# Window attention and expert layer on one core: head loads into spare weight memory, two weight pieces in flight, and a new order of small work

## The chip, the core and the metric

The kernel runs on one core of a Trainium2 chip. The metric is the device time in microseconds (us) of one execution. The core's engines work in parallel, each on its own queue in order: TensorE (PE, matmuls and transposes), VectorE (DVE), ScalarE (ACT), GpSimd (POOL), and SyncE (SP), which here only loads registers and issues DMAs. ACT and POOL issue DMAs too.

## The reference, cut to what matters

Attention over 8 sequences of 576 positions, 8 heads of 64, in which a position sees itself and the 63 before it; its result, 4608 rows of 512, goes through a layer of 8 experts, of which each row uses one.

```python
def _attn_ref(q, k, v):                      # (8, 8, 576, 64)
    scores = (1 / np.sqrt(D)) * q @ k^T
    mask = (rel >= 0) & (rel < 64)           # rel = query position - key position
    attn = softmax(np.where(mask, scores, -1e9))
    return attn @ v

def _moe_ref(x, modality_id, w_gate, modality_bias, w1, w2):   # x (4608, 512)
    logits = x @ w_gate + modality_bias[modality_id]
    e_idx = np.argmax(logits, axis=1)
    gate_w = softmax(logits)[np.arange(N), e_idx]
    for e in range(8):
        h = np.maximum(x[mask_e] @ w1[e], 0)                   # w1[e] (512, 1024)
        out[mask_e] = gate_w[mask_e, None] * (h @ w2[e])       # w2[e] (1024, 512)
```

## The kernel before

**Steps.** The attention is worked through in 36 steps s, each for one pair of 64-row blocks (128 rows); two pairs are a group G. The loop at L917 writes each step out by hand for five engines (`manual_schedule`): what stands first in the loop stands first on its engine's queue. In step s PE does the router's logits of pair s-3, values of s-2, scores of s, transposes of the exponentials of s-1, the transposes of x of s-2, and the transposes of heads of a later group (`heads_t`, group s//2+1: the k heads in an even step, the q heads in an odd one). DVE takes the scores' masked minima (`minima`, L562), copies half of v (`swap_v`, L492), forms the reciprocal of the sums (`sums`, L589 and L590), copies most heads out, adds the bias (L629) and multiplies the values by the reciprocal (`values_out`, L607). ACT takes the exponentials (`exps`, L574, eight a step), copies pT (L583) and xaT (L616) and the second half of the k heads (L524). POOL copies the other half of v (L493) and scatters the finished rows by expert into memory (L700, an indirect DMA).

**Heads.** q and k of a group (512 KB each) are loaded by SP (`load_qk`, L509) into two buffers `qk`; k of group G in step 2G-3, q in 2G-2, used from step 2G-2 on. SP issues in order, so a load that waits for its buffer holds up what stands behind it. v of pair p (256 KB, three buffers) is loaded in step p.

**Table work.** The routing of rows to experts makes short DVE instructions. They stand in two lists, `routing` (of the current group) and `queue` (of the plan of which rows make up a slot), and `tick(n)` issues the next n entries, `routing` first. The third entry of a group's route also issues a small exp on ACT (L647). Each step has four ticks of 4 (of 10 in step 10). `choose` (step 5) picks the two experts whose weights are kept, `plan` (after groups 2, 4, 5, 6, 8, 10, 13, 15) appends 11 or 12 entries that end in the row number of a slot.

**Weights.** Each of two experts X and Y has 32 KB per partition in `Whi` and again in `Wlo`: a weight is split into a rounded part and its rest, and each product is made of three matmuls. `weights(s)` splits the piece loaded last (ACT or POOL copies it into Whi, L108; POOL subtracts into Wlo, L109) and loads the next of 32 pieces of 256 KB into one of two buffers `raw`. It is called once a step before step 12, three times from there on.

**Slots.** From step 12 (`FIRST`) on, pieces of expert work are put between the attention pieces, four `gap`s a step. A slot is 256 rows of one expert, in 16 pieces: `fetch` gets the row number and loads the rows (L196, tile `xt`), `x_part` transposes and splits them (L245, L185, L186), `first` makes the hidden layer (L270, k from 0 to 3), `second` the output (L292), `finish` the scaling (L300) and the indirect store (L303). The next slot is fetched at k == 3 of the current one while attention runs, at k == 2 after it.

Before the loop stand the setup of constants, the first group's heads (`first_heads`, two pairs of blocks i), and `keep_warm`, a few matmuls on zeros.

Of the kernel before, what the change touches and what calls it, by code (L numbers as in the profile page):

```python
# [26 lines left out]
def tile_window_attn_moe(  # L27
# [56 lines left out]

    Whi = wpool.tile([P, 2, 2 * WC], F32R, name="Whi")
    Wlo = wpool.tile([P, 2, 2 * WC], F32R, name="Wlo")

# [17 lines left out]
    def split_piece(raw, buf, c, lo_engine, hi_copy=nc.scalar.copy):  # L105

        cols = slice(c * WCH, (c + 1) * WCH)
        hi_copy(out=Whi[:, buf, cols], in_=raw)  # L108
        lo_engine.tensor_tensor(  # L109
            out=Wlo[:, buf, cols], in0=raw, in1=Whi[:, buf, cols].bitcast(F32), op=ALU.subtract)  # L110

# [120 lines left out]
    def slot_pieces():  # L232
# [26 lines left out]
        def first(sl, k, i):  # L259

            buf = sl["buf"]
            if i == 0:
                sl["hb"] = bank(k % 2)
            hb = sl["hb"]
            hi, lo = sl["x"]
            mm = [(w, c, hi) for c in range(NC1) for w in (Whi, Wlo)] + [(Whi, c, lo) for c in range(NC1)]
            for n, (w, c, x) in enumerate(mm):
                c0 = c * F + (2 * k + i) * P
                ready(sl, c0)
                nc.tensor.matmul(  # L270
                    out=hb[:, i * TP:(i + 1) * TP], lhsT=w[:, buf, c0:c0 + P], rhs=x[:, c * TP:(c + 1) * TP],
                    start=(n == 0), stop=(n == len(mm) - 1))
            if i == 1:
                hh = epool.tile([P, 512], F32R, name="hh", bufs=2)
                hl = epool.tile([P, 512], F32R, name="hl", bufs=2)
                sl["h", k] = hh, hl
                later.append(lambda: (
                    nc.scalar.activation(out=hh, in_=hb, func=AF.Relu),  # L278
                    nc.vector.scalar_tensor_tensor(  # L279
                        out=hl, in0=hb, scalar=0.0, in1=hh.bitcast(F32), op0=ALU.max, op1=ALU.subtract)))  # L280

        def second(sl, k, t):

            buf = sl["buf"]
            if k == 0:
                sl["y", t] = ps_m.tile([P, DM], F32, name=f"y{t}")
            hi, lo = sl["h", k]
            mm = [(h, w, i) for i in range(2) for h, w in ((hi, Whi), (hi, Wlo), (lo, Whi))]
            for n, (h, w, i) in enumerate(mm):
                c0 = WC + (2 * k + i) * DM  # L290
                ready(sl, c0)
                nc.tensor.matmul(  # L292
                    out=sl["y", t], lhsT=h[:, i * TP + t * P:i * TP + (t + 1) * P], rhs=w[:, buf, c0:c0 + DM],
                    start=(k == 0 and n == 0), stop=(k == NK - 1 and n == len(mm) - 1))
            if k == NK - 1:
                later.append(lambda: finish(sl, t))

        def finish(sl, t):
            y = epool.tile([P, DM], F32, name="y", bufs=2)
            nc.vector.tensor_scalar(  # L300
                out=y, in0=sl["y", t], scalar1=sl["gate"][:, t:t + 1], scalar2=None, op0=ALU.mult)
            nc.gpsimd.memset(pause, 0.0)
            ins = nc.gpsimd.indirect_dma_start(  # L303
                out=out, out_offset=bass.IndirectOffsetOnAxis(ap=sl["id"][:, t:t + 1], axis=0),
                in_=y, in_offset=None, bounds_check=N - 1, oob_is_err=False)
            tc.declare_no_dep(ins.ins, group="outs", reason="rows are distinct")
            tc.add_to_no_dep_group("outs", ins.ins)

        def half_first(sl, n):
# [5 lines left out]
            for m, (x, w, c) in enumerate(mm):  # L315
                c0 = c * F + n * 512
                ready(sl, c0)
                nc.tensor.matmul(
                    out=hb, lhsT=x[:, c * P:(c + 1) * P], rhs=w[:, buf, c0:c0 + 512],
                    start=(m == 0), stop=(m == len(mm) - 1))  # L320
# [13 lines left out]
        def half_second(sl, a):  # L334
# [5 lines left out]
            for m, (w, n, c, lo) in enumerate(mm):  # L340
# [3 lines left out]
                    out=yp[:, cols], lhsT=sl["h", n][lo][:, c * P:(c + 1) * P],  # L344
                    rhs=w[:, buf, c0 + cols.start:c0 + cols.stop],
                    start=(m == 0), stop=(m == len(mm) - 1))
# [5 lines left out]
            def out_():  # L352
                y = epool.tile([P, DM], F32, name="y", bufs=2)
                nc.vector.tensor_scalar(
# [104 lines left out]

    PARTS = ((K0, K1), (Q0, Q1))  # L460
    WARM = 4, 3

# [32 lines left out]
    def new_qk(G, nm):  # L495
        qk[G, nm] = work.tile([P, 2, H, D], F32, name="qk", bufs=2)

# [88 lines left out]
    def sums(p):  # L586
        sm = st[p, "s"][2]
        rs = st[p, "rs"] = small.tile([P, H], F32, name="rs")
        nc.vector.tensor_scalar(out=rs, in0=sm, scalar1=1e-9, scalar2=None, op0=ALU.add)  # L589
        nc.vector.reciprocal(out=rs, in_=rs)  # L590

# [194 lines left out]

    spare = epool.tile([P, DM], F32, name="y", bufs=2)
    mod_i = spare[0:NPR, 0:2 * P].bitcast(I32)
# [20 lines left out]
    nc.gpsimd.memset(kT[:, :, RING - 1, :], 0.0)  # L809
    warm = const.tile([1, 1], F32, name="warm")  # L810
    nc.vector.memset(warm, 0.0)
    nc.scalar.activation(out=warm, in_=warm, func=AF.Exp)

# [61 lines left out]
    padrow = epool.tile([P, 2, ROW], F32, name="xt")  # L875
    spare2 = epool.tile([P, DM], F32, name="y", bufs=2)
    nc.gpsimd.memset(padrow, 0.0)
# [21 lines left out]

    for i in range(GB):  # L900
        for nm in "kq":
            first_heads(nm, i, turn_bank(0), nc.vector.tensor_copy if nm == "k" else nc.scalar.copy)
        if i == 0:
            keep_warm(WARM[1])
    by_bias = []

    def weights(s):

        if raws:
            raw, x, c = raws.pop(0)  # L910
            split_piece(raw, x, c, nc.gpsimd, nc.scalar.copy if s >= FIRST else nc.gpsimd.tensor_copy)
        if pieces:
            x, c = pieces.pop(0)
            raw = epool.tile([P, WCH], F32, name="raw", bufs=2)
            raws.append((load_piece(raw, evs[x], c), x, c))

    for s in range(NPR + 4):  # L917
# [30 lines left out]
        run_later()  # L948
        tick(n_tick)
        if s < NPR:  # L950
# [31 lines left out]
        run_later()  # L982
        tick(n_tick)
        if s == 0:
# [277 lines left out]
```

## Time and profile before

| | us |
|---|---|
| median of 3 runs | 665.7 (664.6 to 666.95) |
| the profiled execution | 664.81 |
| its span | 663.1 |
| PE busy | 627.0 |
| DVE, ACT, POOL busy | 361.9, 298.1, 166.5 |

The span goes from the first to the last instruction on the core. A busy engine is one with an instruction under way; matmuls overlap, so a share of 95% isn't 95% of what PE could do. The rows in the next sections come from the page, from groups of instructions by line ("busy, mean ns of one | idle before"), from tables of waits ("engine, line waited for: us in total, times, longest us"), from the timeline ("start, length, engine, line, operation", and in brackets the idle time of the engine just before), from the chain of work that ended last, and from busy time by stage.

### The profile page before, as it was taken

The numbers are of one execution on the slowest core, as the hardware profiler recorded it, in microseconds if no ns is written. First come the engines' busy times: TensorE is split into PE (matmuls) and PEld (weight loads), VectorE is DVE, ScalarE is ACT, GpSimd is POOL, SyncE is SP. The second block draws the span as 40 slices with busy tenths as digits, with TensorE's granted clock in tenths as the row PEclk, the third lists the DMA queues.
The fourth block names the chain that finished last, engine by engine and source line by source line (L and its number), as shares of the span: only waits on it lengthen the run. The fifth ranks groups of instructions, "written<-read, shape, count | busy, mean of one in ns | idle before, by whom it ended". The sixth has DMA issues, their size and how long they took to land.

```text
span 663.1 us, 17266 instructions
## 1 busy us (share of the span) xinstructions
PE 627.0 (95%) x6508; PEld 559.6 (84%) x6508; DVE 361.9 (55%) x1465; ACT 298.1 (45%) x928; POOL 166.5 (25%) x314
## 2 busy tenths in 40 slices
PE   6887688899999999999999999999999999999996
PEld 4776578688888998999898988999999899999986
DVE  2689974657766676655765563222222634566611
ACT  2687747557666655455555111111111523555511
POOL 4303623535555032122230410110011011011102
PEclk9999988899999999999999999999999999999999
DMA  7957974666687463646422216411050651677400
GB/s 121 201 112 164 223 173 115 174 160 178 175 214 170 100 160 86 140 112 146 112 85 64 97 49 208 160 63 49 17 191 24 177 183 46 216 247 228 137 1 35
DMA packets 138885, 88.07 MB, mean 133 GB/s; under 512 B 116746, under 2 KB 116784, under 8 KB 138672
## 3 DMA queue, kind: packets, MB, share of 16 engines
q1 hardware_dynamic: 130112, 67.44, 41.8%
q0 software_dynamic: 5856, 18.92, 7.9%
q10 hardware_dynamic: 2832, 0.59, 0.7%
q8 instruction: 52, 0.85, 0.6%
q14 instruction: 33, 0.27, 0.1%
HBM read 67.49 MB, written 23.91 MB: 138 GB/s over the span
## 4 chain that ended last, share of the span: by engine, by line
PE 83%; DVE 5%; ACT 4%; DMA 4%; issue 2%; POOL 1%; SPq 1%; POOLq 0%; ACTq 0%; DVEq 0%
PE y L292 30%; PE em L270 20%; PE sp L270 10%; PE tp L430 8%; PE sp L548 5%; PE av L600 4%; PE tp L624 3%; ACT ss L574 2%; DMA qk<-in_k_dram 2%; DVE ss L562 2%; PE y L343 1%; PE em L245 1%; PE tp L245 1%; DMA xt<-xs_scratch 1%; DMA qk<-in_q_dram 0%
## 5 line engine op out<-in xcount | busy, mean ns | idle before, releaser
L292 PE MATMUL y<-Whi,hh 128*128 128x512 f32 x288 | 119.5, 415 | 0.7 <-ACT Whi L108 0.7
L292 PE MATMUL y<-Wlo,hh 128*128 128x512 f32 x288 | 113.7, 395 | 2.5 <-POOL Wlo L109 2.5
L292 PE MATMUL y<-Whi,hl 128*128 128x512 f32 x288 | 113.3, 394 | 0.0
L574 ACT ACTIVATE ss<-ss,mn 128x128 f32<-128x128 f32 x288 | 112.4, 396 | 1.8 <-DVE mn L562 1.8
L270 PE MATMUL em<-xh,Whi 128*128 128x256 f32 x392 | 101.7, 293 | 2.5 <-ACT xh L185 1.9
L270 PE MATMUL em<-xh,Wlo 128*128 128x256 f32 x392 | 96.8, 280 | 0.0
L303 POOL DMA_INDIRECT out_dram<-y,id x36 | 37.2, 1032 | 204.7 <-DVE y L300 167.1
L279 DVE SCALAR_TENSOR_TENSOR hl<-em,hh 128x512 fp32r<-128x512 f32 x49 | 33.8, 690 | 91.4 <-ACT hh L278 88.8
L270 PEld LDWEIGHTS em<-xh,Whi 128*128 128x128 f32 x392 | 74.4, 190 | 3.9 <-ACT xh L185 2.1
L270 PEld LDWEIGHTS em<-xh,Wlo 128*128 128x128 f32 x392 | 74.4, 190 | 0.9
L562 DVE CUSTOM_DVE_ANT_0 ss<-sp,masks 128x128 f32<-128x128 f32 x288 | 63.6, 286 | 14.7 <-PE sp L548 14.3
L583 ACT COPY pT<-tp 128x512 f32<-128x512 f32 x58 | 31.5, 590 | 83.7 <-PE tp L430 83.7
L278 ACT ACTIVATE hh<-em 128x512 fp32r<-128x512 f32 x49 | 29.0, 593 | 87.3 <-PE em L270 87.3
L292 PEld LDWEIGHTS y<-Whi,hl 128*128 128x128 f32 x288 | 54.4, 189 | 12.4
L292 PEld LDWEIGHTS y<-Wlo,hh 128*128 128x128 f32 x288 | 54.6, 190 | 10.6 <-POOL Wlo L109 3.5
L270 PE MATMUL em<-xl,Whi 128*128 128x256 f32 x392 | 62.3, 281 | 0.0
L292 PEld LDWEIGHTS y<-Whi,hh 128*128 128x128 f32 x288 | 54.4, 189 | 8.9 <-ACT Whi L108 1.4
L700 POOL DMA_INDIRECT xs_scratch<-xa,idx x36 | 35.5, 986 | 96.2 <-DVE idx L712 26.3
L574 ACT ACTIVATION_READ_ACCUMULATOR ss<-ss,mn 128x1 f32 x288 | 55.6, 193 | 0.0
L109 POOL TENSOR_TENSOR Wlo<-raw,Whi 128x512 fp32r<-128x512 f32 x32 | 41.0, 1281 | 51.5 <-ACT Whi L108 47.7
L270 PEld LDWEIGHTS em<-xl,Whi 128*128 128x128 f32 x392 | 53.1, 190 | 0.0
L279 DVE SCALAR_TENSOR_TENSOR hl<-sp,hh 128x512 fp32r<-128x512 f32 x23 | 15.9, 692 | 66.2 <-ACT hh L278 66.2
(233 smaller groups left out, 1277.6 us busy)
## 6 DMA issues: line engine op xcount, KB each, us to landing
xt<-xs_scratch SPq DMA_DIRECT2D x18, 514.0 KB, 4.2
vo<-in_v_dram SPq DMA_DIRECT2D x32, 256.0 KB, 5.1
raw<-in_moe_w_dram SPq DMA_DIRECT2D x32, 256.0 KB, 4.0
vo<-in_moe_w_dram SPq DMA_DIRECT2D x24, 256.0 KB, 3.6
ss<-in_moe_w_dram SPq DMA_DIRECT2D x24, 256.0 KB, 3.6
qk<-in_k_dram SPq DMA_DIRECT2D x22, 256.0 KB, 4.8
qk<-in_q_dram SPq DMA_DIRECT2D x22, 256.0 KB, 4.1
xs_scratch<-xs_scratch SPq DMA_DIRECT2D x8, 514.0 KB, 6.2
```

The lines of the kernel that those rows point to most:

```text
L109: lo_engine.tensor_tensor(out=Wlo[:, buf, cols], in0=raw, in1=Whi[:, buf, cols].bitcast(F32), op=ALU.subtract)
L270: nc.tensor.matmul(out=hb[:, i * TP:(i + 1) * TP], lhsT=w[:, buf, c0:c0 + P], rhs=x[:, c * TP:(c + 1) * TP], start=(n == 0), stop=(n == le ...
L278: nc.scalar.activation(out=hh, in_=hb, func=AF.Relu),
L279: nc.vector.scalar_tensor_tensor(out=hl, in0=hb, scalar=0.0, in1=hh.bitcast(F32), op0=ALU.max, op1=ALU.subtract)))
L292: nc.tensor.matmul(out=sl["y", t], lhsT=h[:, i * TP + t * P:i * TP + (t + 1) * P], rhs=w[:, buf, c0:c0 + DM], start=(k == 0 and n == 0), s ...
L303: ins = nc.gpsimd.indirect_dma_start(out=out, out_offset=bass.IndirectOffsetOnAxis(ap=sl["id"][:, t:t + 1], axis=0), in_=y, in_offset=None ...
L430: nc.tensor.transpose(out=out_, in_=in_, identity=ident[p0:p0 + n, p0:p0 + n])
L548: nc.tensor.matmul(out=sp[a][c * W64:(c + 1) * W64, hp * P:(hp + 1) * P], lhsT=qT[rows, hp, g + c, :], rhs=kT[rows, hp, win[c], :], start= ...
L562: nc.vector.tensor_tensor_reduce(out=ss[a][:, hp, :], in0=sp[a][:, hp * P:(hp + 1) * P], in1=mask, scale=-1.0 / 8.0, scalar=3.0e38, op0=AL ...
L574: nc.scalar.activation(out=ss[a][:, hp, :], in_=ss[a][:, hp, :], func=AF.Exp, bias=mn[:, h:h + 1], scale=-1.0, accum_out=sm[:, h:h + 1])
L583: nc.scalar.copy(out=pT, in_=pp)
L700: ins = nc.gpsimd.indirect_dma_start(out=xs, out_offset=bass.IndirectOffsetOnAxis(ap=idx[:, j:j + 1], axis=0), in_=xg[j], in_offset=None)
```

## The change

- `Whi` and `Wlo` become two tiles each. Until the first piece of expert Y is split, the room of Y's Whi is a tile `stock`; q and k of groups 1 to 4 are loaded into its eight parts. k and q of groups 1 to 5 are now both loaded in step G-2.
- `weights(s)` keeps two pieces under way, and splits one when two are there. `raw` and the output tile `y` share four buffers.
- The sums' small addition goes to POOL, the reciprocal to `values_out`, a step later.
- The first tick of a step stands before exps(0, 1); the last one issues 8 before step 12 and is gone from there on.
- The table load for the exponentials stands earlier in the setup; the second pair of blocks of the first group is transposed after scores(0), behind the warm matmuls.
- A slot from the second on is fetched at k == 2 during attention as well.

```diff
-    Whi = wpool.tile([P, 2, 2 * WC], F32R, name="Whi")
-    Wlo = wpool.tile([P, 2, 2 * WC], F32R, name="Wlo")
+    stock = wpool.tile([P, 2 * WC], F32, name="Whi1")
+    Whi = [wpool.tile([P, 2 * WC], F32R, name="Whi0"), None]
+    Wlo = [wpool.tile([P, 2 * WC], F32R, name=f"Wlo{x}") for x in range(2)]
...
     def split_piece(raw, buf, c, lo_engine, hi_copy=nc.scalar.copy):
-        hi_copy(out=Whi[:, buf, cols], in_=raw)
+        if Whi[buf] is None:
+            Whi[buf] = wpool.tile([P, 2 * WC], F32R, name="Whi1")
+        hi_copy(out=Whi[buf][:, cols], in_=raw)
...
-                if k == 3 and nxt is None or k == 2 and last:
+                if nxt is None and (k == 3 or k == 2 and position[0] > SLOT_PIECES):
                     assert todo
                     nxt = fetch()
...
+    AHEAD = 1, 2, 3, 4
...
     def new_qk(G, nm):
-        qk[G, nm] = work.tile([P, 2, H, D], F32, name="qk", bufs=2)
+        if G in AHEAD:
+            n = 2 * H * D
+            i = 2 * AHEAD.index(G) + "kq".index(nm)
+            qk[G, nm] = stock[:, i * n:(i + 1) * n].rearrange("p (t h d) -> p t h d", t=2, d=D)
+        else:
+            qk[G, nm] = work.tile([P, 2, H, D], F32, name="qk", bufs=2)
...
     def sums(p):
-        nc.vector.tensor_scalar(out=rs, in0=sm, scalar1=1e-9, scalar2=None, op0=ALU.add)
-        nc.vector.reciprocal(out=rs, in_=rs)
+        nc.gpsimd.tensor_scalar(out=rs, in0=sm, scalar1=1e-9, scalar2=None, op0=ALU.add)
...
     def values_out(p):
         rs = st.pop((p, "rs"))
+        nc.vector.reciprocal(out=rs, in_=rs)
...
     for G in range(1, NG):
-        for nm, step in (("k", max(2 * G - 3, 0)), ("q", 2 * G - 2)):
+        ahead = G <= AHEAD[-1] + 1
+        for nm, step in (("k", G - 2 if ahead else 2 * G - 3), ("q", G - 2 if ahead else 2 * G - 2)):
...
+    warm = const.tile([1, 1], F32, name="warm")
+    nc.vector.memset(warm, 0.0)
+    nc.scalar.activation(out=warm, in_=warm, func=AF.Exp)
-    spare = epool.tile([P, DM], F32, name="y", bufs=2)
+    spare = epool.tile([P, DM], F32, name="y", bufs=4)
...
-    for i in range(GB):
+    def first_pair(i):
         for nm in "kq":
             first_heads(nm, i, turn_bank(0), nc.vector.tensor_copy if nm == "k" else nc.scalar.copy)
-        if i == 0:
-            keep_warm(WARM[1])
+    first_pair(0)
...
     def weights(s):
-        if raws:
+        if len(raws) == 2 or raws and not pieces:
             raw, x, c = raws.pop(0)
             split_piece(raw, x, c, nc.gpsimd, nc.scalar.copy if s >= FIRST else nc.gpsimd.tensor_copy)
-        if pieces:
+        while pieces and len(raws) < 2:
             x, c = pieces.pop(0)
-            raw = epool.tile([P, WCH], F32, name="raw", bufs=2)
+            raw = epool.tile([P, WCH], F32, name="y", bufs=4)
             raws.append((load_piece(raw, evs[x], c), x, c))
...
             scores(s)
+            if s == 0:
+                keep_warm(WARM[1])
+                first_pair(1)
             minima(s)
...
             sums(s - 1)
+        tick(n_tick)
         if s < NPR:
             exps(s, (0, 1))
...
         run_later()
-        tick(n_tick)
         if s < NPR:
             exps(s, (2, 3, 4))
...
         run_later()
-        tick(n_tick)
+        if s < FIRST:
+            tick(8)
```

More of the change, by code (lines that the diff above doesn't have):

```diff
@@ L107, in split_piece @@
         cols = slice(c * WCH, (c + 1) * WCH)
-        hi_copy(out=Whi[:, buf, cols], in_=raw)
+        if Whi[buf] is None:
+            Whi[buf] = wpool.tile([P, 2 * WC], F32R, name="Whi1")
+        hi_copy(out=Whi[buf][:, cols], in_=raw)
         lo_engine.tensor_tensor(
-            out=Wlo[:, buf, cols], in0=raw, in1=Whi[:, buf, cols].bitcast(F32), op=ALU.subtract)
+            out=Wlo[buf][:, cols], in0=raw, in1=Whi[buf][:, cols].bitcast(F32), op=ALU.subtract)
     queue = []
@@ L318, in half_first @@
                 nc.tensor.matmul(
[L319 removed]
+                    out=hb, lhsT=x[:, c * P:(c + 1) * P], rhs=w[buf][:, c0:c0 + 512],
                     start=(m == 0), stop=(m == len(mm) - 1))
```

15 lines of the change are left out of this document (6 added, 9 removed).

## The prediction

> **What bounds the kernel now.** I read the page first (part 1, the engines' shares of the span), then the busy time by stage, because a share over the whole span hides where TensorE (PE) is not the limit.
>
> ```profile
> PE 627.0 (95%) x6508; PEld 559.6 (84%) x6508; DVE 361.9 (55%) x1465; ACT 298.1 (45%) x928; POOL 166.5 (25%) x314
> ```
>
> ```profile
> 0.00:20.00 20.00, 13.87 (x114) 9.41 (x115) 4.39 (x23) 6.49 (x21) 9.45 (x54) 1.00 0.81 130
> 20.00:40.00 20.00, 16.57 (x300) 14.59 (x299) 16.12 (x91) 15.43 (x62) 4.18 (x7) 1.00 0.91 178
> ...
> 80.00:100.00 20.00, 13.98 (x211) 11.90 (x211) 15.78 (x75) 10.80 (x44) 7.01 (x10) 0.83 0.75 186
> ...
> 160.00:180.00 20.00, 20.00 (x256) 18.00 (x259) 15.46 (x75) 13.28 (x46) 10.96 (x12) 1.00 0.64 174
> ...
> 600.00:663.00 63.00, 57.97 (x376) 52.15 (x374) 26.08 (x41) 18.82 (x34) 10.16 (x19) 0.99 0.31 97
> ```
>
> Columns: stretch, length, busy PE, PE weight load, DVE, ACT, POOL, granted PE clock, DMA share, GB/s. PE is idle 36.1 us in all (663.1 - 627.0); 5.0 of them lie in the last stretch, which the change leaves alone, and from 160 to 600 it is full. So the prize is some 30 us of idle PE before 160, where the attention steps run alone (s below 12, to about 95) and the first expert weights arrive. Nothing that only lightens DVE, ACT or SP after 160 shortens the span. Which waits make up the idle time there is told by the table of waits, cut to PE, for 0 to 20, 20 to 100, and 95 to 160:
>
> ```profile
> PE tp L430 <- DMA qk<-in_k_dram: 3.5, 2, 1.8
> PE y L430 <- DMA qk<-in_k_dram: 1.3, 2, 0.7
> ```
>
> ```profile
> PE tp L624 <- DVE e_n L149: 5.4, 1, 5.4
> PE sp L548 <- ACT kT L524: 3.6, 4, 1.4
> ```
>
> ```profile
> PE y L292 <- POOL Wlo L109: 2.5, 3, 0.8
> ...
> PE tp L430 <- DVE lg L629: 1.0, 1, 1.0
> ```
>
> The head loads (qk) hold PE only before 16 us; after that the scores wait for ACT's copy into kT, once for one DVE queue at step 10 (5.4), and later for weights that are split just in time.
>
> **The change, part by part.** Times are against the profiled execution's 664.81 us (span 663.1, 1.7 around it); the median shown is 665.7, 0.9 above it. I add the same difference to the median. Gains are negative.
>
> *First scores sooner.*
>
> ```profile
> 8.76 1.46 PE L801 MATMUL em<-hh 128*128 128x512 bf16 x3
> ...
> 12.18 1.99 PE L548 MATMUL sp<-kT,qT 64*64 64x128 f32 x32
> ...
> 14.34 0.29 DVE L562 CUSTOM_DVE_ANT_0 ss<-sp,masks 128x128 f32<-128x128 f32 x1 [2.21 <-PE sp L548]
> ...
> 17.82 0.63 ACT L524 COPY kT<-tp 128x512 f32<-128x512 f32 x1
> 17.90 1.98 PE L548 MATMUL sp<-kT,qT 64*64 64x128 f32 x32
> ```
>
> scores(0) can start when the first pair's q copy is out (ACT's copy of it runs from 8.87 to 9.48 in the timeline) instead of at 12.18. But the three warm matmuls (1.46), the second pair's transposes (about 1.0 for k) and its DVE copy (0.69) are now issued between scores(0) and the minima: 9.5 + 2.0 + 1.46 + 1.0 + 0.7 = 14.6, against 14.34. The exps and ACT's kT copy behind them (17.82) move no sooner, and scores(1) waits for that copy. So the loads that land early save PE its 1.3, and ACT sets the time. Bounds: -1.7 (the clock comes up one or two of its periods earlier, so that transposes and scores take about half; scores took 1.98 here and 1.06 at 49.03 in the chain) and +0.3. I take **-0.6**.
>
> *Heads ahead.* Groups 1 to 4 get own room, so their loads no longer wait for a buffer. Past 20 us no PE wait on qk is left to remove: 0. What is new is a crowd: up to step 3 SP now issues six groups of 1 MB, 1 MB of v and 0.5 MB of pad rows, 7.5 MB, the v rows of step 3 last. At 178 GB/s (20 to 40, share 0.91) that takes 42 us from 1.6, so v of step 3 lands at 43.7 while POOL copies it at 41.07; at the 223 GB/s below it lands at 35.
>
> ```profile
> 25.00:30.00 5.00, 4.33 (x80) 3.92 (x82) 3.85 (x22) 3.70 (x15) 1.21 (x2) 1.00 1.10 223
> ```
> ```profile
> 41.07 0.61 POOL L493 COPY ve<-vo 64x512 f32<-64x512 f32 x1 [6.12 <-DVE wn L648]
> ```
>
> Bounds 0 and +2.6; I take 0, nearer the rate of the full stretch.
>
> *Sums on POOL, reciprocal later.* Two DVE instructions leave the place behind the ve copy.
>
> ```profile
> L589 DVE TENSOR_SCALAR rs<-sm 128x8 f32<-128x8 f32 x36 | 10.6, 293 | 1.1
> L590 DVE RECIPROCAL rs<-rs 128x8 f32<-128x8 f32 x36 | 7.3, 203 | 1.2
> ```
>
> The reciprocal comes back ahead of the xa multiply, so DVE gets 0.3 per step, and 0.5 for what hangs on the place behind ve. POOL's add isn't in the trace; the gate copy of 128x2 takes POOL 0.21 and the 128x36 tensor_scalar at 18.30 takes 0.33, so 0.2 to 0.35 on an engine 25% busy. Behind it wait POOL's scatters and splits; its reader is one step later. It hides. Step 1 is a DVE chain (minima, rs, bias table, two qT copies): **-0.4**. Of the odd steps, 3 and 5 are ACT and PE chains (0); 7, 9 and 11 have rs in the chain of waits, each limited to 0.2 to 0.4 by PE's scores right behind: **-0.9** (0 to -1.5). At step 10 the kT copy that PE waits 5.4 for stands behind rs (0.47), the reciprocal (0.20) and ten table instructions; the ten stay: **-0.65**.
>
> *Table work before the exps.* For s below 12 no DVE instruction changes place by this; what moves is on ACT. In even steps the four table entries hold ACT's small exp of the router (ex), and it now stands ahead of exps(0,1) and of the xaT copy, which filled ACT's wait so far.
>
> ```profile
> 40.16 0.17 DVE L589 TENSOR_SCALAR rs<-sm 128x8 f32<-128x8 f32 x1
> 40.37 0.20 DVE L590 RECIPROCAL rs<-rs 128x8 f32<-128x8 f32 x1
> 40.48 0.12 DVE L643 TENSOR_REDUCE lm<-lg 128x2 f32<-128x16 f32 x1
> 40.64 0.17 DVE L644 TENSOR_TENSOR lg<-lg,lm 128x16 f32<-128x16 f32 x1
> ```
> ```profile
> 38.47 1.08 ACT L583 COPY pT<-y 128x512 f32<-128x512 f32 x2 [1.02 <-PE y L430]
> ...
> 40.21 0.58 ACT L616 COPY xaT<-tp 128x512 f32<-128x512 f32 x1
> 40.84 0.22 ACT L647 ACTIVATE ex<-lg 128x16 f32<-128x16 f32 x1
> ...
> 43.28 0.59 ACT L524 COPY kT<-em 128x512 f32<-128x512 f32 x1
> ```
>
> Step 4: without rs, lg is ready at 40.16 + 0.33 = 40.5. ACT, free of pT at 39.5, now idles until then; then ex 0.13, two exps 0.77, xaT 0.49, six exps 2.31 (40.97 to 43.28), kT at 44.2 instead of 43.28: +0.9, and PE's scores wait for kT (the 3.6 above). Steps 6 and 8: 0.67 saved on DVE, 1.26 put behind ex: +0.6 each. **+2.1** (0 to +3). Steps 12 and 14: ACT's wait only changes place, **-0.2**.
>
> *Fewer ticks from step 12 on.* Two leftovers of one route now run first in the next step, and the tick at the step's end is gone. At step 17 PE waits for lg behind such table work (0.99); without it **-1.0**.
>
> ```profile
> 159.85 0.66 PE L430 MATMUL tp<-ident_r,ss 128*128 128x128 f32 x4 [0.99 <-DVE lg L629]
> ```
>
> But the plan of step 13 (11 entries) is thinned: four in step 14, four in step 15, the rest by the fetch there. So the row number for slot 1 comes in step 15.
>
> ```profile
> 129.02 0.16 DVE L132 TENSOR_SCALAR rows<-e_at 1x2 int32<-1x2 f32 x1
> ...
> 135.38 0.29 DVE L562 CUSTOM_DVE_ANT_0 ss<-sp,masks 128x128 f32<-128x128 f32 x1 [0.32 <-PE sp L548]
> ...
> 137.19 0.42 DVE L492 COPY ve<-vo 64x512 f32<-64x512 f32 x1
> ```
> ```profile
> 133.17 0.38 SPq L196 DMA_DIRECT2D xt<-xs_scratch  x1
> ```
> ```profile
> 142.87 0.54 PE L245 MATMUL em<-ident_r,xt 128*128 128x128 f32 x4
> ```
> ```profile
> 182.82 4.97 DMA xt<-xs_scratch
> ```
>
> Six entries of 0.19 behind 137.64 give 138.8; SP needs some 0.9 to load the number and issue (181.90 to 182.82 in the chain at step 19), the transfer 4.2 (median on the page) to 4.97: it lands at 143.9 to 144.7, while PE wants it at 142.87. A new wait, 1.0 to 1.8, **+1.4**; the raw loads queued behind it on SP have a call more of slack than before. For later slots the fetch is one k sooner, with rows long known: the wait of 0.5 on xt at 187.9 goes, **-0.5**.
>
> *Two pieces under way.* Each piece is loaded one call sooner and split in the same call as before. ACT's waits on raw go, but PE's waits for Whi and Wlo follow splits that start without a DMA wait (124.43 is behind an exp): 0. If the splits were late by DMA it would be worth up to the 2.5 + 0.7 of those waits. The separate tiles and y's four buffers cost nothing.
>
> Sum: -0.6 - 0.4 - 0.9 - 0.65 + 2.1 - 0.2 - 1.0 + 1.4 - 0.5 = **-0.75**: 664.06 against the profiled run, 664.95 against the median; I give 664.9.
>
> **Rivals.** The clock decides the first two.
>
> ```profile
> 80.00:84.00 4.00, 0.35 (x8) 0.39 (x9) 3.73 (x13) 2.75 (x13) 2.93 (x5) 0.66 0.50 156
> 84.00:88.00 4.00, 4.00 (x77) 3.87 (x76) 2.31 (x7) 0.00 (x0) 1.15 (x2) 0.50 0.18 11
> ...
> 124.00:128.00 4.00, 2.17 (x8) 0.86 (x6) 2.93 (x10) 3.19 (x13) 2.00 (x2) 1.00 0.56 166
> 128.00:132.00 4.00, 3.41 (x11) 2.84 (x12) 1.07 (x5) 1.13 (x2) 1.03 (x2) 0.64 0.47 140
> ```
>
> *Faster by the clock.* The stall at step 10 is followed by half clock until about 88.8: logits, values and scores run from 83.64 to 88.36, where three such sets take 2.6 (92.33 to 94.91 in the chain), a loss of 2.1. If the shorter stall falls differently and keeps the clock, and the start warms early (-1.1 more): 661.7; with ACT's new order costing nothing as well: 659.6. For: the dip follows a stall that the change shortens. Against: 0.65 of 5.4 is little.
>
> *Slower by the late slot.* If the table entries of step 15 collide with POOL's splits as e_at did (1.13 at 158.43), the stall before L245 is 3.3 instead of 1.4, and a dip as at 129.8 follows, 1.5 to 2.1 more: 664.95 + 1.9 + 1.8 = 668.6. [...] For: the DVE queue shows such collisions; against: POOL is idle until 140 there.
> The rows above bear the dip out: at 124 to 128 PE was busy 2.17 of 4 us, with no gap over 0.9, and the clock fell to 0.64 after it. Without a dip this rival ends at 664.95 + 1.9 = 666.9, no measurable change.
> [...]
>
> *Nothing that counts, or late values.* The loads were hidden past 16 us anyway; with v of step 3 late by 2.6: 667.5.
>
> **How the numbers follow.** About 0.3% (2 us) can be told from no change. Forecast 0.42 (of it 0.12 faster, 0.28 same, 0.02 slower); faster by the clock 0.30; late slot 0.18, of it 0.15 with the dip (slower) and 0.03 without (same); hidden or late values 0.10, half same, half slower. Together 0.42 faster, 0.36 same, 0.22 slower. The range runs from 658.5 (clock and ACT's order both kind) to 670 (late slot, and half of the late values): 658.5 to 670.
>
> **What would show it.** Minima of step 0 no sooner than 14.2; ex with an idle ACT ahead of it in steps 4, 6, 8, and kT's copy later against the minima; rs gone from DVE; PE waiting on xt at L245 near 143, and no 0.99 on lg near 160; qk gone from PE's waits. Wrong if the steps to 95 got shorter by over 3 us, if the half-clock rows are fewer or more, or if PE's idle time after 160 changes.

## The result, and the profile after

The changed kernel is slower by 0.9%: median 672.9 us (668.55 to 675.49, 20 executions) against 665.62 for the kernel before on the same chip, ratio 1.009, interval [1.0069, 1.0111]. By the ratio that is 6.0 us (4.6 to 7.4); the ratio uses all executions and isn't the quotient of the two medians, which would give 1.011. The 20 executions fall into two groups, eight of 668.55 to 670.5 and twelve of 672.84 to 675.49. The profiled one took 668.81, so it is of the faster group: its span is 667.1, 4.0 above that of before, and what the slower group loses beyond that is not in these rows. Chips differ (below), so only the ratio to the kernel before on the same chip is compared from here on; a ratio is turned into us by multiplying its difference from 1 with the time of before there. One execution of a later version ("before, sums on POOL") took 1015.78 at a granted clock of 0.56, and its ratio is of the 12 others.

The page's first part for the changed kernel (engine, busy time, share of the span, instructions):

```profile
PE 626.3 (94%) x6508; PEld 559.8 (84%) x6508; DVE 356.6 (53%) x1429; ACT 296.8 (44%) x928; POOL 178.2 (27%) x350
```

PE's work is what it was (627.0); the 36 additions have gone from DVE to POOL. What grew is idle PE: 36.1 before, 667.1 - 626.3 = 40.8 now. Busy time by stage tells where (columns as in the prediction), first the changed kernel, then the one stage of before that the prediction doesn't show:

```profile
20.00:40.00 20.00, 15.94 (x284) 14.05 (x283) 13.83 (x74) 14.01 (x58) 3.56 (x8) 0.91 1.12 213
40.00:60.00 20.00, 14.21 (x258) 12.86 (x258) 14.65 (x87) 13.50 (x55) 5.79 (x11) 0.91 0.42 98
...
160.00:180.00 20.00, 18.61 (x263) 16.70 (x263) 15.16 (x68) 11.45 (x40) 11.44 (x15) 1.00 0.84 213
```
```profile
40.00:60.00 20.00, 15.91 (x309) 13.73 (x307) 17.21 (x100) 15.52 (x64) 4.53 (x8) 1.00 0.69 148
```

From 40 to 60 PE is busy 1.7 less, and the granted clock, 1.00 from 20 to 60 before, is 0.91 in both stages. The DMA share shows the loads bunched: 1.12 and then 0.42, where it was 0.91 and 0.69. The same instruction in each step, the multiplication that forms xa, gives the account by step (start in us):

| step | 2 | 3 | 4 | 5 | 8 | 9 | 12 | 15 | 16 | 17 | 18 |
|---|---|---|---|---|---|---|---|---|---|---|---|
| before | 24.88 | 30.36 | 36.88 | 42.53 | 62.79 | 69.28 | 93.95 | 134.36 | 147.18 | 159.72 | 169.21 |
| after | 24.73 | 31.64 | 38.16 | 46.94 | 67.04 | 74.13 | 98.07 | 138.52 | 151.58 | 165.16 | 174.37 |
| difference | -0.2 | +1.3 | +1.3 | +4.4 | +4.3 | +4.9 | +4.1 | +4.2 | +4.4 | +5.4 | +5.2 |

Two places hold the loss: 2 to 3 (+1.4) and 4 to 5 (+3.1). What step 17 adds (+1.0) doesn't last: the difference is +6.7 in step 19, +3.8 in step 20 and +4.4 in step 36, as it was in step 16. PE's waits between 20 and 100, in the changed kernel and then in the kernel before (engine, line, what it waited for: total, times, longest):

```profile
PE y L635 <- ACT xaT L627: 4.7, 3, 2.1
...
PE tp L635 <- ACT xaT L627: 4.2, 4, 2.4
PE av L610 <- POOL ve L498: 2.9, 2, 2.1
PE sp L558 <- ACT kT L534: 1.6, 3, 0.6
```
```profile
PE tp L624 <- ACT xaT L616: 2.5, 4, 0.7
PE y L624 <- ACT xaT L616: 1.9, 3, 0.7
PE av L600 <- POOL ve L493: 0.8, 1, 0.8
```

Lines have moved by 4 to 11 in the rows shown. The waits for xaT rose by 4.5 and those for ve by 2.1, while the wait for kT, which the forecast saw rising, fell by 2.0. Step 4 shows both new waits; the timeline of the changed kernel for ACT, PE, POOL and DVE there:

```profile
41.96 0.22 ACT L658 ACTIVATE ex<-lg 128x16 f32<-128x16 f32 x1 [1.14 <-DVE lg L655]
...
42.85 0.56 ACT L627 COPY xaT<-tp 128x512 f32<-128x512 f32 x1
...
45.64 0.60 ACT L534 COPY kT<-em 128x512 f32<-128x512 f32 x1
```
```profile
43.47 0.64 PE L635 MATMUL y<-wg,xaT 128*64 128x8 f32 x16 [2.01 <-ACT xaT L627]
44.90 0.37 PE L610 MATMUL av<-ve,pT 128*64 128x64 f32 x1 [0.79 <-POOL ve L498]
```
```profile
44.24 0.60 POOL L498 COPY ve<-vo 64x512 f32<-64x512 f32 x1 [7.65 <-PE y L635]
44.92 0.23 POOL L599 TENSOR_SCALAR rs<-sm 128x8 f32<-128x8 f32 x1
```
```profile
45.19 0.20 DVE L616 RECIPROCAL rs<-rs 128x8 f32<-128x8 f32 x1 [0.87 <-POOL rs L599]
```

ACT stands idle 1.14 for the router's lg, then does ex, two exps and only then xaT, for which PE waits 2.01. Then PE waits 0.79 more for POOL's copy of v. The row names a PE instruction as what released that copy, but the copy reads nothing of it. It needs v of pair 3, issued at 37.92; v takes 3.1 to 6.0 from issue to landing by its tile's rows, so it can have landed as late as 43.9. With ex back in its place ("ex behind" below, heads still loaded ahead), the same copy starts at 43.90, for a v issued at 37.76, and there the row names the transfer:

```profile
43.90 0.60 POOL L498 COPY ve<-vo 64x512 f32<-64x512 f32 x1 [7.18 <-DMA vo<-in_v_dram]
```

So the copy waited for v, in the changed kernel most likely too. POOL's add stands behind that copy, so it is late too, and DVE waits for it.

v is late from the start. SP's queue, POOL and PE of the changed kernel:

```profile
16.56 0.90 SPq L484 DMA_DIRECT2D vo<-in_v_dram  x1
...
24.21 2.97 SPq L519 DMA_DIRECT2D Whi<-in_k_dram  x4
27.23 3.54 SPq L519 DMA_DIRECT2D Whi<-in_q_dram  x4
30.81 0.62 SPq L484 DMA_DIRECT2D vo<-in_v_dram  x1
...
37.92 0.89 SPq L484 DMA_DIRECT2D vo<-in_v_dram  x1
```
```profile
22.57 0.60 POOL L498 COPY ve<-vo 64x512 f32<-64x512 f32 x1 [1.77 <-DMA vo<-in_v_dram]
```
```profile
23.23 0.27 PE L610 MATMUL av<-ve,pT 128*64 128x64 f32 x1 [2.09 <-POOL ve L498]
```

A step's heads keep SP's queue busy for 6.5 us (24.21 to 30.77), and v stands behind them. PE's 2.09 is in step 2, for the ve that POOL makes in step 1 from v of pair 0; before, the same wait is the 0.8 above.

The stalls of 2.09 and 2.01 each have half clock behind them. Four stretches of 3.4 us of the changed kernel (columns as above), then two of before at the corresponding places:

```profile
20.40:23.80 3.40, 1.31 (x25) 1.07 (x25) 3.10 (x18) 3.40 (x17) 1.25 (x3) 1.00 1.06 204
23.90:27.30 3.40, 3.40 (x54) 2.95 (x49) 1.68 (x8) 0.11 (x2) 0.00 (x0) 0.50 1.03 219
41.20:44.60 3.40, 0.90 (x19) 0.57 (x17) 2.03 (x9) 2.64 (x13) 0.36 (x1) 0.97 0.83 164
44.70:48.10 3.40, 3.20 (x63) 3.09 (x64) 0.89 (x2) 1.54 (x7) 1.40 (x5) 0.54 0.04 8
```
```profile
20.40:23.80 3.40, 2.58 (x49) 2.27 (x51) 3.12 (x23) 3.28 (x15) 1.96 (x4) 1.00 0.97 195
...
38.00:41.40 3.40, 2.74 (x38) 2.50 (x38) 3.20 (x24) 2.87 (x11) 0.33 (x1) 1.00 0.54 80
```

PE busy 1.31 or 0.90 of 3.4 us, with no single gap over 2.1, was followed by half clock, from 23.9 to 27.3 and from 44.4 to 47.8, 3.41 us each; in the two stretches of before, with 2.58 and 2.74 busy, the clock stayed at 1.00. The other half-clock stretches of the two traces up to 200 are 3.41 long as well (three in the changed kernel, two in the kernel before), but for the 6.83 from 81.3 to 88.2 before. A single stall of this length isn't always followed by one: behind 2.42 at 58.82 and 2.10 at 72.44 the changed kernel's clock stayed at 1.00. The mean granted clock goes with the two groups of executions: 0.983 to 0.989 in the eight faster ones, 0.971 to 0.978 in the twelve slower ones.

### The profile page after: what moved, and what is told of

Read it like the earlier page. It is cut to its first block, busy times and chain, and to the rows that moved or that the text cites. A ratio compares the mean times of both kernels' runs of the same rounds, so it can differ in the third digit from the quotient of the medians.

```text
span 667.1 us, 17273 instructions
## 1 busy us (share of the span) xinstructions
PE 626.3 (94%) x6508; PEld 559.8 (84%) x6508; DVE 356.6 (53%) x1429; ACT 296.8 (44%) x928; POOL 178.2 (27%) x350
## 4 chain that ended last, share of the span: by engine, by line
PE 74%; ACT 0%; DVE 0%; issue 0%; POOL 0%; POOLq 0%; ACTq 0%
PE y L296 28%; PE em L274 18%; PE sp L274 10%; PE tp L434 7%; PE av L610 3%; PE sp L558 3%; PE tp L635 2%; PE y L347 1%; PE tp L249 1%; PE em L249 1%; PE sp L322 0%; PE em L322 0%; ACT ss L584 0%; DVE hl L283 0%; POOL out_dram L360 0%
## 5 line engine op out<-in xcount | busy, mean ns | idle before, releaser
L584 ACT ACTIVATE ss<-ss,mn 128x128 f32<-128x128 f32 x288 | 112.5, 397 | 0.0
L296 PEld LDWEIGHTS y<-Whi,hl 128*128 128x128 f32 x288 | 54.4, 189 | 12.2
L584 ACT ACTIVATION_READ_ACCUMULATOR ss<-ss,mn 128x1 f32 x288 | 55.8, 194 | 0.0
L113 POOL TENSOR_TENSOR Wlo<-y,Whi 128x512 fp32r<-128x512 f32 x32 | 40.8, 1291 | 36.8 <-ACT Whi L112 36.4
```

Source lines behind the costliest of these rows:

```text
L113: lo_engine.tensor_tensor(out=Wlo[buf][:, cols], in0=raw, in1=Whi[buf][:, cols].bitcast(F32), op=ALU.subtract)
L296: nc.tensor.matmul(out=sl["y", t], lhsT=h[:, i * TP + t * P:i * TP + (t + 1) * P], rhs=w[buf][:, c0:c0 + DM], start=(k == 0 and n == 0), s ...
L584: nc.scalar.activation(out=ss[a][:, hp, :], in_=ss[a][:, hp, :], func=AF.Exp, bias=mn[:, h:h + 1], scale=-1.0, accum_out=sm[:, h:h + 1])
```

## The experiments

The theory after these rows: two parts cost time, **ex** on ACT ahead of exps(0, 1) and xaT, and **v queued behind 1 MB of heads** a step, each by a wait of PE and the half clock behind it; the rest gains about what the forecast gave it. The main rival: the clock alone makes the loss, and whichever small stall starts the dips is accidental.

### Undoing the two parts

**ex behind** (the changed kernel, only below step 12 with the first tick in its old place):

```diff
             sums(s - 1)
-        tick(n_tick)
+        if s >= FIRST:
+            tick(n_tick)
         if s < NPR:
             exps(s, (0, 1))
...
         run_later()
+        if s < FIRST:
+            tick(n_tick)
```

> The kernel after, with the first tick of steps 0 to 11 put back behind the x transposes, so that ACT's router exp stands again behind exps(0, 1) and xaT. Theory A (ex's place costs 0.6 to 0.9 in steps 4, 6 and 8, and the longer idle time of PE some half-clock periods more): 2 to 3.5 us faster than the kernel after's 672.9, ratio to before about 1.005. Rival B (only the late values count): no change, 1.009. Rival C (the thinned table work from step 12 on): 1.009.

**Loads as before** (the room of their own is kept; only the steps are the old ones):

```diff
-        for nm, step in (("k", G - 2 if ahead else 2 * G - 3), ("q", G - 2 if ahead else 2 * G - 2)):
+        for nm, step in (("k", max(2 * G - 3, 0)), ("q", 2 * G - 2)):
```

> The kernel after, with the heads of groups 1 to 5 loaded in the steps of before (k in 2G-3, q in 2G-2), still into their own room. Theory B (v queues behind 1 MB of heads a step; PE waits 0.6 in step 1 and 2.1 in step 4 for values, and half-clock periods follow): 3 to 5 us faster than after, ratio about 1.003; the waits of POOL's ve copy on vo fall to those of before. Rival A: no change, 1.009; the early loads are then worth something and it is slower.

(In the rows above the two waits for values are 2.09 in step 2 and 0.79 in step 4.)

**Both** edits together:

> Both edits together. If A and B hold and add up: 5.5 to 8 us faster than after, ratio 0.998 to 1.001. If the cause lies from step 12 on (C): 1.007 to 1.009. If the two share one cost, the clock: little more than the better of the two alone.

**Filler**: the changed kernel with eight matmuls of 384 columns on constants added ahead of the router's in steps 3 to 11; their result goes to an unused part of a bank, so that the output isn't touched.

```diff
         xaT = st.pop((p, "xT"))
+        if p + 3 < FIRST:
+            for _ in range(8):
+                nc.tensor.matmul(
+                    out=lt[:, P:512], lhsT=ones, rhs=ones[:, None, :].broadcast_to([P, 3, P]), start=True, stop=True)
```

> The kernel after, with 8 matmuls of 384 columns on constants ahead of each router matmul of steps 3 to 11, into the unused columns of its bank: about 1.3 us of PE work a step at full clock where PE waited for xaT for up to 2.4. They add nothing to the output. Theory D (most of the 7 us is half clock, which follows PE's idle stretches): the granted clock goes from 0.975 to 0.985 or more and the time falls by 2 to 4 us, ratio 1.004. If the waits themselves are the cost: 1.009 to 1.02, since the work is added where there was no wait.

(The 1.3 us a step is an estimate: before, four of the matmuls of 512 columns at the start take 1.89 us and three 1.46, so 0.43 each; eight of 384 make 2.6, and about half of that at the later rate, where a set of scores takes 1.06 instead of 1.98.)

| against before (665.07) | median | ratio | interval | us |
|---|---|---|---|---|
| ex behind | 666.8 | 1.0017 | [1.0, 1.0034] | +1.1 |
| loads as before | 667.61 | 1.0025 | [0.9999, 1.0051] | +1.7 |
| both | 662.51 | 0.9961 | [0.9947, 0.9976] | -2.6 |
| filler | 671.87 | 1.0097 | [1.0066, 1.0128] | +6.5 |

Against the +6.0 of the whole change, undoing the place of ex gains 4.9 and undoing the order of the loads 4.3; undone second, they gain 4.3 and 3.7. Together it is 8.6, so within these intervals (each some 2 wide to either side for a difference) they add up. Without both the rest gains 2.6. The 12 executions of "loads as before" fall into two groups of six, 664.23 to 666.81 at a clock of 0.989 to 0.991 and 668.4 to 670.44 at 0.975 to 0.981, so what ex costs hangs on the clock as well; its profile, 670.37, is of the slower group. PE's waits from 20 to 100 keep the two apart; with ex behind, then with the loads as before:

```profile
PE av L610 <- POOL ve L498: 4.0, 2, 2.3
...
PE tp L635 <- ACT xaT L627: 2.5, 4, 0.7
PE y L635 <- ACT xaT L627: 1.9, 3, 0.7
```
```profile
PE y L635 <- ACT xaT L627: 5.1, 3, 2.5
...
PE tp L635 <- ACT xaT L627: 4.2, 4, 2.4
```

With ex behind, the xaT waits are those of before to the tenth, and ve is still late. With the loads as before the waits for xaT stay and no wait for ve is left. With both edits the router's waits for xaT are those of before and 0.2 is left for ve; one transposition now waits 2.2 for xaT.

The filler shows how much of the loss in step 4 is clock. The stage from 40 to 60 in its run:

```profile
40.00:60.00 20.00, 16.98 (x275) 14.11 (x275) 15.25 (x89) 13.41 (x53) 5.78 (x11) 1.00 0.41 96
```

The clock is 1.00 there instead of 0.91. From xa of step 4 to xa of step 5 it takes 8.0 us, where the changed kernel takes 8.8 and the kernel before 5.7: keeping the clock gave back 0.8 of the 3.1, and PE still waits for xaT (0.7) and for ve (0.85) there. From step 7 to step 11 the filler's trace is 3.9 slower than the changed kernel's, so in all nothing was gained. The waits themselves are thus the larger part in step 4, and the rival that the clock alone makes the loss doesn't fit there; one run with one size of filler doesn't say what a better placed one would do.

### One part alone, and what the two edits hide

The next four ran on a chip where the kernel before takes 673.48. **v first**: ex behind, heads ahead as in the change, but the loads of v listed ahead of them within the step:

```diff
+    for p in range(NPR):
+        when(p, load_v, p)
     for G in range(1, NG):
         ahead = G <= AHEAD[-1] + 1
...
-    for p in range(NPR):
-        when(p, load_v, p)
```

> The first edit (router exp behind xaT again), and the heads still loaded ahead, but v of a step issued before the heads of that step. If only the place of v in SP's queue made the early loads costly: as fast as both edits, 662.5, or faster by what the early loads are worth. If the crowd of transfers itself slows v, the first transposes or the pad rows: between 663 and 666.8.

**Pair as before**: both edits, and the first group's second pair and the warm matmuls back ahead of the loop.

> Both edits, and the second pair of blocks transposed before scores(0) again, behind the warm matmuls. If PE's earlier full clock and the sooner scores are worth what step 1 shows (0.65): 663.2. If they are worth nothing behind ACT's kT copy: 662.5.

**Ticks as before**: loads as before, and all ticks of all steps in their old places and numbers.

> Heads loaded as before, and all ticks of a step as before, those from step 12 on too. If the thinned table work pays (the forecast's 1.0 at step 17, against 1.4 for the late slot): within 1 us of 662.5. If it is what makes both edits beat the kernel before: 665.

**ex ahead in the kernel before**, the one part alone:

```diff
             sums(s - 1)
+        if s < FIRST:
+            tick(n_tick)
         if s < NPR:
             exps(s, (0, 1))
...
         run_later()
-        tick(n_tick)
+        if s >= FIRST:
+            tick(n_tick)
```

> The kernel before with one edit alone: the first tick of steps 0 to 11 ahead of exps(0, 1). Theory A, now with the 6.1 that undoing it was worth in the kernel after: 3 to 6 us slower than before, ratio 1.005 to 1.009, and PE's waits on xaT up by some 4.5 us. By the forecast's own reading: 0.9 + 0.6 + 0.6 less nothing, since rs stays on DVE: 2 us, 1.003.

| against before (673.48) | median | ratio | interval | us |
|---|---|---|---|---|
| v first | 664.91 | 0.9869 | [0.9839, 0.9898] | -8.8 |
| pair as before | 664.14 | 0.9856 | [0.9828, 0.9885] | -9.7 |
| ticks as before | 667.48 | 0.9907 | [0.9876, 0.9938] | -6.3 |
| ex ahead, alone | 684.15 | 1.0126 | [1.0082, 1.0171] | +8.5 |

v first and the loads of before (in "pair as before") come out alike: no cost or gain of loading heads ahead is seen once v goes first. The part alone in the kernel before costs 8.5 (5.5 to 11.5; 3 to 6 were expected), with the same new waits, 11.6 in the two rows against 4.4 in the trace of before:

```profile
PE y L624 <- ACT xaT L616: 6.8, 3, 4.2
...
PE tp L624 <- ACT xaT L616: 4.8, 4, 3.1
```

The new numbers of the ticks are worth some 3 (-9.7 against -6.3). The two kernels also differ in the first pair and in the last tick of the steps below 12, and their intervals overlap, so the size is rough. Their traces are 1.6 apart in step 21 and 5.0 at the end, and there only the ticks differ. In step 22 the scores take 2.67 us (212.15 to 214.82) with the old ticks and 1.10 with the new ones. PE's waits in "ticks as before" name no engine for it ("issue" is time in which PE waited for nothing that the profile shows):

```profile
PE sp L558 <- issue: 0.8, 3, 0.3
```

The trace of the kernel before, on another chip, has the old ticks and no such row.

### Another chip, and a better version

On a third chip (before: 675.68) the changed kernel and the version with both edits ran again:

> The kernel after, unchanged, on the chip of the three runs beside it: the reference point for them, since the kernel before took 665.1 on one chip and 673.5 on another. If the chips differ for the kernel before alone, after is 668 to 675 on any of them and the ratio follows the kernel before: 1.009 where that takes 665, 0.99 to 1.0 where it takes 673.

> Both edits again (router exp behind xaT in steps 0 to 11, heads loaded as before), on the same chip as the kernel after: 8 to 11 us faster than after if the result of the first four runs holds on any chip.

with them **sums on DVE** (both edits, and the add and the reciprocal in their old place) and **four entries in step 10** (both edits, and n_tick 4 there instead of 10):

```diff
     def sums(p):
-        nc.gpsimd.tensor_scalar(out=rs, in0=sm, scalar1=1e-9, scalar2=None, op0=ALU.add)
+        nc.vector.tensor_scalar(out=rs, in0=sm, scalar1=1e-9, scalar2=None, op0=ALU.add)
+        nc.vector.reciprocal(out=rs, in_=rs)
...
     def values_out(p):
-        nc.vector.reciprocal(out=rs, in_=rs)
```
```diff
-        n_tick = 10 if s == FIRST - 2 else 4
+        n_tick = 4
```

> Both edits, and the sums' addition and the reciprocal back on DVE in their old place. By the forecast's terms (0.4 in step 1, 0.9 in steps 7, 9, 11, 0.65 in step 10): 2 us slower than both edits. If DVE's old place in the chain never decided: no difference.

> Both edits, and 4 entries a tick in step 10 too instead of 10, so that the k heads' copy there waits for four table instructions and not ten; the rest of the entries follow behind it. PE's wait on that copy falls from 4.6 to about 2 us, and the half-clock period behind it (about 89 to 93) should go: 2.5 to 4.5 us faster than both edits alone. If the row number of the first slot is then late, the gain is given back in step 12: no difference.

| against before (675.68) | median | ratio | interval | us |
|---|---|---|---|---|
| changed, again | 678.86 | 1.0026 | [0.9994, 1.0058] | +1.8 |
| both, again | 664.97 | 0.9846 | [0.9819, 0.9874] | -10.4 |
| both, sums on DVE | 671.85 | 0.9951 | [0.9926, 0.9976] | -3.3 |
| both, four entries | 663.28 | 0.982 | [0.9794, 0.9846] | -12.2 |

The changed kernel, too, is slower on this chip than the 668 to 675 that was expected. Here the two parts cost 12.2 (+1.8 against -10.4), and the sums' place 7 where 2 was forecast. Four entries in step 10 gave 1.8 more, less than the forecast of 2.5 to 4.5 for that run, and the two intervals overlap: the wait for e_n goes, and PE waits 2.7 for an exponential (L584) in its place.

The changed kernel's two traces tell something of the chip. They differ by 10.0 in span, and 9.5 of that is there by step 13; from 180 on PE's stages agree to 0.2. First the stage from 60 to 80 in the trace used so far, then on this chip:

```profile
60.00:80.00 20.00, 15.73 (x317) 13.79 (x314) 15.54 (x92) 15.19 (x61) 8.42 (x14) 1.00 0.58 140
```
```profile
60.00:80.00 20.00, 15.37 (x243) 14.19 (x245) 13.11 (x73) 12.41 (x54) 6.10 (x10) 0.76 0.57 133
```

So this chip is not slower in everything; it shows more half clock in the steps that run alone. One trace is of the faster group of its chip's executions and the other of the slower, so part of the 10.0 is that.

The traces with the sums on POOL and on DVE (662.61 and 672.72) are 1.5 apart up to step 8, 4.2 in step 9, 7.7 in step 12 and 10.0 in the end. Step 8 shows how it begins. DVE's queue with the sums on POOL, then with the sums on DVE:

```profile
63.61 0.42 DVE L497 COPY ve<-vo 64x512 f32<-64x512 f32 x1
...
64.27 0.26 DVE L655 TENSOR_TENSOR lg<-lg,lm 128x16 f32<-128x16 f32 x1
...
64.86 0.68 DVE L534 COPY kT<-em 128x512 f32<-128x512 f32 x1
```
```profile
64.92 1.47 DVE L497 COPY ve<-vo 64x512 f32<-64x512 f32 x1
...
67.19 1.05 DVE L655 TENSOR_TENSOR lg<-lg,lm 128x16 f32<-128x16 f32 x1
...
68.96 0.68 DVE L534 COPY kT<-em 128x512 f32<-128x512 f32 x1
```

The chain, which starts 1.3 later, runs beside POOL's work (a scatter from 64.51 to 65.47, the subtraction of a split from 66.94 to 68.21); it stretches from 1.25 to 4.0 up to the kT copy, and the clock is at half behind it, where the other trace has 1.00. Two stretches of 2 us of the run with the sums on DVE:

```profile
70.00:72.00 2.00, 1.48 (x25) 0.75 (x18) 1.55 (x4) 1.29 (x6) 0.80 (x2) 0.50 1.20 221
72.00:74.00 2.00, 2.00 (x14) 2.00 (x11) 1.69 (x15) 0.58 (x1) 0.00 (x0) 0.50 0.24 71
```

That DVE is slowed by POOL's work at the same time is read from the overlap; it wasn't tried by itself, and the later steps weren't followed.

What was left: does the sums' gain belong to them alone, and where does the kernel before lose its 8 to 10 us on the second and third chips? The last three versions were the kernel **before, again**; the kernel **before with the sums on POOL** (the change's edit of `sums` and `values_out` alone); and **v first with four entries** (v first, and n_tick 4 in step 10).

> The kernel before, unchanged, for its trace on the chip of this batch. If the chip is one of those where it takes 673 to 676 us, the theory of DVE's place (the kernels with add and reciprocal on DVE are 7 to 10 us slower there) expects PE's idle time ahead of 160 to be larger than the 31 us of the profiled execution shown at the start by about as much as the time is, at waits on rs, kT, ve or lg in the steps that run alone, with half-clock rows where the first profile has none. The rival, that the chip is slower in everything, expects the busy time of PE to be larger by as much, and the waits as they were.

> The kernel before with one part of the change alone: the add of 1e-9 on POOL and the reciprocal on DVE ahead of the xa multiply. Theory (the sums' place is what the slower chips pay for): on a chip where before takes 673 to 676 it gains 5 to 9 us, and on one where before takes 665 it gains 0 to 2 (forecast: 1.95). Rival (the gain of 6.9 came only together with the other parts): under 2 us on either.

> The kernel after with the first tick below step 12 back behind x_t, v issued ahead of the heads that it shares a step with, and four table entries in step 10 in place of ten. Theory: loading ahead is worth nothing by itself once v goes first, so it equals the version with the loads of before and four entries, 0.982 of before on a chip where before takes 675, within 1 us. Rival: heads ahead in own room save SP waits, and it is 1 us or more faster.

| against before (665.6) | median | ratio | interval | us |
|---|---|---|---|---|
| before, again | 666.33 | 1.0006 | [0.9989, 1.0023] | +0.4 |
| before, sums on POOL | 663.66 | 0.998 | [0.9965, 0.9995] | -1.3 |
| v first, four entries | 661.04 | 0.9943 | [0.9922, 0.9964] | -3.8 |

The kernel before took here what it took on the first chip, so where it loses time on the other two stays open; its mean granted clock is 0.983 and 0.984 there and 0.988 here. The sums alone gain 1.3 (0.3 to 2.3) here, near the forecast (1.95); there is no usable trace of that run, and the 7 of the other chip were not tried alone there. v first with four entries gains most where before takes 665 (-3.8, interval -5.2 to -2.4, against -2.6, -3.5 to -1.6, with both edits; the two overlap); heads ahead still show no gain of their own. The versions to keep: both edits (0.9961 and 0.9846 on two chips), with four entries (0.982), and v first with four entries (0.9943).

## Why the prediction was wrong

Its number was 664.9, no measurable change, by a sum of -0.75; it gave 0.42 to faster, 0.36 to no change and 0.22 to slower. Measured was +6.0, a median of 672.9, above the upper end of its range (670). Two terms hold the miss: without ex ahead and with the loads as before the rest measured -2.6, and the terms of the rest sum to -0.6 - 0.4 - 0.9 - 0.65 - 0.2 - 1.0 + 1.4 - 0.5 = -2.85. That agreement is in part luck: single terms of it were off by one to two either way, as told below, and on the second and third chips the same rest measured about -10.

**"Heads ahead: bounds 0 and +2.6; I take 0" is the step that failed**: it put this term at nothing, and it measured 4.3 (3.7 when undone second). The mechanism stood there, v of step 3 last of 7.5 MB in SP's queue, landing between 35 and 43.7, with POOL's copy wanting it at 41.07. The copy came at 44.24, past the late end. The slow bound was the right one, and the 0 had been taken by the fast one: the changed kernel moved 213 GB/s from 20 to 40, but 99 to 200 before that, 189 on average up to 45. And the step asked only about step 3: v of step 0, issued at 16.56 instead of 14.52, made PE wait 2.09 in step 2 instead of 0.8. What a load is moved in front of must be asked for every step in which it is moved. "Late values" had been given a chance of 0.10, half of it slower, and a price of 2.6 without any clock.

**"Table work before the exps: +2.1" was mis-sized**: 4.9 (8.5 alone on the second chip). The order of events in step 4 came as written: ACT idle until lg, ex, two exps, xaT, and ACT's kT copy 2.4 later, of which 1.3 had come before the step (0.9 was forecast). But the forecast took PE's wait for that kT copy as the price. PE waits for xaT much earlier in the step (2.01), which the sum never asked; and kT's wait went down. The reader of a copy that is moved back is the first to look for, not the last one on its engine.

**The clock** was left out of the sum and put into rivals. Nothing of it happened at L245; at step 10 the half clock went from 6.83 us to 3.41, but the kernel was still 4.1 later in step 12, after 4.9 in step 9. Dips came behind the new stalls instead, at 23.9 and 44.4; at 24.59 a set of scores took 1.99 instead of some 1.06. "Slower by the late slot" had the wrong place: slot 1's rows were issued at 143.73, in a step that itself was 4.2 later, and PE waited 0.4, not 1.4:

```profile
143.73 0.39 SPq L200 DMA_DIRECT2D xt<-xs_scratch  x1
```
```profile
PE em L249 <- DMA xt<-xs_scratch: 0.4, 1, 0.4
```

**"Step 17: -1.0"** didn't come; step 17 itself is 1.0 longer. Another table instruction of DVE stands there now and takes 2.39 beside three splits on POOL, and PE waits 1.39 for lg instead of 0.99. DVE, POOL, PE of the changed kernel:

```profile
161.14 2.39 DVE L136 TENSOR_SCALAR e_f_i<-cnt 1x8 int32<-1x8 f32 x1
```
```profile
159.71 3.79 POOL L113 TENSOR_TENSOR Wlo<-y,Whi 128x512 fp32r<-128x512 f32 x3
```
```profile
165.01 0.66 PE L434 MATMUL tp<-ident_r,ss 128*128 128x128 f32 x4 [1.39 <-DVE lg L640]
```

The forecast had -1.0 + 1.4 - 0.5 = -0.1 for the late steps, and from step 16 to step 36 the difference between the traces doesn't change; but of the three terms only the last came (no wait on xt stands behind 160 any more, before 0.5), so this sum is right by luck.

**First scores sooner, -0.6**: right in mechanism. The minima of step 0 came no sooner, and the start gained 0.65 up to step 1's minima, at 19.29 instead of 19.94, since PE was faster by then: 16 of step 1's scores took 0.67 from 17.08, where all 32 took 1.98 from 17.90 before. (The granted clock reads 1.00 from 0 to 20 in both traces, so only the durations show it. The forecast's -1.7 fits half of a half-clock stretch of 3.41.)

```profile
14.65 0.28 DVE L572 CUSTOM_DVE_ANT_0 ss<-sp,masks 128x128 f32<-128x128 f32 x1
...
19.29 0.29 DVE L572 CUSTOM_DVE_ANT_0 ss<-sp,masks 128x128 f32<-128x128 f32 x1 [2.17 <-PE sp L558]
```

Late v then took it back at once; over the whole kernel, the version with the old start ran as well on the second chip (0.9856, against 0.9869 for v first), so no gain of it is shown.

**Sums on POOL, -1.95**: alone on the last chip the measured -1.3 (-0.3 to -2.3) agrees with it; on the third, beside both edits, it was much too small (-7).

**Two pieces under way, 0**: not tried alone, and neither were the earlier fetch and the shared buffers. From 100 to 200 PE waits 3.0 for Wlo and 0.6 for Whi, before 2.5 and 0.7, which agrees with 0.

## What to carry to other kernels

When a load is moved ahead, list what stands behind it on its queue in every step that it is moved to, and issue what is wanted first, first: here the wrong order cost some 4 us, and listing v first within the step was as good as not moving the heads at all. When a small instruction that waits for another engine is put ahead of a copy in an in-order queue, price the first reader of that copy. And where PE is the bound with little slack, price a new stall of 2 us with the half clock that may follow it (here 3.41 us of it behind 2.09 and 2.01, none behind 2.42 and 2.10); the one attempt here to buy the clock back with idle work gained nothing.

## What the runs showed that was not expected

- The kernel before takes 665.07 and 665.6 on two batches' chips and 673.48 and 675.68 on two others, while the versions with both edits take 662.51 to 664.97 on all of the first three. The answer on the change depends on it: +0.9% on one chip, +0.3% [-0.1%, +0.6%] on the third. The cause isn't settled; on the third a half-clock dip at step 8 came with the sums on DVE, and not without. Waits of PE for nothing that the profile shows (0.4 to 2.1 us in all from 20 to 640) stand in five of the eight traces from these two slower chips and in none of the eight usable ones from the others; but the changed kernel's trace on the third has none and is 10 us longer, so they are at most a part.
- 3.41 us of half clock followed where PE was busy 0.9 to 1.3 of 3.4 us, though no gap exceeded 2.1.
- Executions of one kernel on one chip fall into two groups some 4 us apart, with a lower granted clock in the slower one (the changed kernel, and loads as before). What decides between them isn't known.
- Short DVE instructions took up to 2.39 us where POOL split weights at the time: e_f_i on 1x8 0.15 to 2.39, the subtraction that makes lg 0.26 in one trace and 1.05 in the other.
- Filler on PE raised the granted clock from 0.91 to 1.00 from 40 to 60 and gained nothing in all (+6.5 against +6.0).
